# Sums on VectorE, products on GpSimd, and a shared ring of snapshots in a tuned RWKV-5 and SwiGLU kernel

## The chip, the cores and the metric

The kernel runs on one core of one Trainium2 chip. The metric is device time in microseconds (us) of one execution, lower is better. Each run below was judged against runs of the kernel before on the same chip, interleaved with it.

Engines are named as in the profile: PE is TensorE's matmul, PEld its weight load, DVE is VectorE, ACT is ScalarE, POOL is GpSimd, SP is SyncE.

## The reference

RWKV-5 attention over 4 batches, 8 heads, 768 tokens, head size 48, followed by a SwiGLU feed-forward block of width 384 to 1536 to 384 over the 3072 tokens:

```python
for t in range(S):                       # attention: one state per batch and head
    cur = u * k_t (outer) v_t
    y[t] = r_t @ (state + cur)
    state = w * state + k_t (outer) v_t
x = y.transpose(0, 2, 1, 3).reshape(B * S, H * D)
g = x @ w_gate
out = (g * sigmoid(g) * (x @ w_val)) @ w_out
```

(The einsums are written in words here.) The three weight matrices arrive as float64, which the kernel rounds to float32 itself.

## The kernel before

The tokens are cut into 24 units of 128. A unit `s` of the attention has `own_product` (r times k times u, on GpSimd) and `own_sum` (its sum over the head, on VectorE), which give the diagonal of a matrix `At`; `scale` makes the decayed k and r (`khat`, `rhat`), `turn` transposes them, `scores` fills `At`, `outputs` gives x, and `update` renews the state. While the first units run, 18 chunks of weights are rounded: ScalarE makes `w_mag` and `w_low`, VectorE joins sign and magnitude, GpSimd adds `w_low`.

```python
def round_pool():
    ...
    pool.tensor_tensor(dst, dst, low, ALU.add)

def own_product(i):
    kl, rl = k_ld[i % 2], r_ld[i % 2]
    rk = two.tile([P, H, D], FP32, name="rk", tag="rk")     # two buffers
    pool.tensor_mul(rk[:], rl[:], kl[:])
    pool.tensor_mul(rk[:], rk[:], ub[:])
    rks[i] = rk

def own_sum(i):
    dus[i] = three.tile([P, H], FP32, name="du", tag="du")
    dve.tensor_reduce(dus[i][:], rks.pop(i)[:], axis=AX.X, op=ALU.add)
```

The feed-forward block has two forms. The first four units go through plain matmuls into `gv` (gate and value). The rest goes, four units at a time, through a fast 2 by 2 matrix product that has seven block products instead of eight. It needs sums of its inputs (`s` of the weights, `hs` of the hidden activations `hT`), and copies of a PSUM accumulator taken between two products that are added up in it. Those copies are the **snapshots** `p1`, `u2` and `u3`; `c_a` and `c_b` are the accumulators of the first matmul of the block, `o_a` and `o_b` those of the second.

```python
def h_sums(g, n, by):                    # by: the engine
    h11, h12, h21, h22 = h_quarters(g)
    t = three.tile([P, 2, FH, P], FP32, name="hs", tag="w_bits")
    if n == 0:
        by.tensor_add(t[:, 0], h22, h21)
        by.tensor_sub(t[:, 1], t[:, 0], h11)
    else:
        by.tensor_sub(t[:, 0], h11, h21)
        by.tensor_sub(t[:, 1], h12, x["s"][1])
...
# four(g, f, what): one step of the first matmul, for one f of 128 hidden columns
if what in ("p1", "p6", "p7"):
    nm = {"p1": "p1", "p6": "u2", "p7": "u3"}[what]
    x[nm, f] = two.tile([P, 2 * P], FP32, name=nm, tag=nm)  # two buffers each
    act.copy(x[nm, f][:], ps)
...
if what == "h1":
    dve.tensor_mul(h[1], h[1], x.pop(("sg1", f))[:])
    dve.tensor_mul(h[1], h[1], x.pop(("u3", f))[:])         # last reader of u3
...
# two_projections: two of the four pairs of sums on GpSimd
if (j, p) in ((0, 1), (0, 2)):
    h_sums(g, p - 1, dve)
elif (j, p) in ((1, 1), (0, 3)):
    h_sums(g + 1, p // 3, pool)
```

The stage loop, with `gaps` filling in matmuls of the feed-forward block and the rounding of weights:

```python
for s in range(3, N + 2):
    if s + 1 < N:
        own_product(s + 1)
        scale(s + 1)
    if s < N:
        turn(s)
    gaps(s, 0)
    ...  # scores(s - 1), outputs(s - 2)
    if s < N:
        own_sum(s)
        diagonal(s)
    ...  # update(s - 2)
```

Of the kernel before, what the change touches and what calls it, by code (L numbers as in the profile page):

```python
# [15 lines left out]
P = 128  # L16
# [6 lines left out]
def fast(  # L23
# [33 lines left out]
    CC, FC = DM // P, DFF // P  # L57

    cst = ctx.enter_context(tc.tile_pool(name="cst", bufs=1))
    two = ctx.enter_context(tc.tile_pool(name="two", bufs=2))  # L60
    three = ctx.enter_context(tc.tile_pool(name="three", bufs=3))
    ps_a = ctx.enter_context(tc.tile_pool(name="ps_a", bufs=4, space=bass.MemoryType.PSUM))
    ps_w = ctx.enter_context(tc.tile_pool(name="ps_w", bufs=1, space=bass.MemoryType.PSUM))
    ps_f = ctx.enter_context(tc.tile_pool(name="ps_f", bufs=2, space=bass.MemoryType.PSUM))
# [135 lines left out]

    def own_product(i):
        kl, rl = k_ld[i % 2], r_ld[i % 2]
        rk = two.tile([P, H, D], FP32, name="rk", tag="rk")
        pool.tensor_mul(rk[:], rl[:], kl[:])
        pool.tensor_mul(rk[:], rk[:], ub[:])
        rks[i] = rk

    def own_sum(i):
        dus[i] = three.tile([P, H], FP32, name="du", tag="du")
        dve.tensor_reduce(dus[i][:], rks.pop(i)[:], axis=AX.X, op=ALU.add)  # L210


    sg0 = two.tile([P, 1], FP32, name="sg0", tag="sg0")
# [30 lines left out]
    for step, base in ((-64, 0), (64, D - 1)):  # L244
        pool.affine_select(
            out=own[:], in_=own[:], compare_op=ALU.is_ge, fill=0.0,
            base=base, pattern=[[step, 2]], channel_multiplier=1 if step < 0 else -1,
        )
    dve.tensor_scalar(held[:], wcol[:], W_LOW, W_HIGH, ALU.max, ALU.min)
    dve.tensor_copy(sq[:, 0, :], held[:])  # L250
    for l in range(1, 8):
# [4 lines left out]
    for l in range(7):  # L256
        n = 1 << l
        f = sq[:, l, :].unsqueeze(2).to_broadcast([P, HP, n])
        dve.tensor_mul(pw[:, :, P - 2 * n : P - n], pw[:, :, P - n : P], f)
    for n in (1, 0):  # L260
        t_ps = ps_a.tile([P, HP, P], FP32, name="t_ps", tag="a")
        for a in range(HP):
            pe.transpose(t_ps[:, a, :], pw[:, a, n : n + P], ident[:])
        x = t_ps[:].rearrange("p a (e x) -> p (a e) x", e=2)[:, :, 0:D]
        if n:
            act.copy(kscale[:], x)
        else:
            dve.reciprocal(rscale[:], x)
    own_product(0)
    own_product(1)  # L270
    own_sum(0)
    own_sum(1)

    pool.memset(mask[:], 1.0)
    pool.affine_select(
        out=mask[:], in_=mask[:], compare_op=ALU.is_gt, fill=0.0,
        base=0, pattern=[[1, P]], channel_multiplier=-1,
    )

    turned = {}  # L280
    small = deque()

    def scale(i):
        pool.tensor_mul(khat[i % 4][:, :, 0:D], k_ld[i % 2][:], kscale[:])
        pool.tensor_mul(rhat[i % 2][:, :, 0:D], r_ld[i % 2][:], rscale[:])
        if i >= 2:
            load_v(i)
        if i + 2 < N:
            load(i + 2)

    def diagonal(i):

        du = dus.pop(i)
        if i < 2:
            pool.tensor_mul(
                At[i][:], ident[:].unsqueeze(1).to_broadcast([P, H, P]),
                du[:].unsqueeze(2).to_broadcast([P, H, P]),
            )
        else:
            small.extend(  # L300
                lambda h=h: act.activation(  # L301
                    At[i % 2][:, h, :], ident[:], AF.Identity, scale=du[:, h : h + 1]
                )
                for h in range(H)
            )
# [84 lines left out]
    def gate_value(g, f):  # L390
        if f == 0:
            hT[g] = two.tile([P, FC, 2 * P], FP32, name="hT", tag="hT")
        gv = ps_f.tile([P, 2, 2 * P], FP32, name="gv", tag="gv")
        for o, wt in enumerate((wg, wv)):
            for c in range(CC):
                pe.matmul(  # L396
                    gv[:, o, :].rearrange("p (i t) -> p i t", i=2),
                    wt[:, c, P * f : P * (f + 1)], xT[:, 2 * g % NX : 2 * g % NX + 2, c, :],
                    start=(c == 0), stop=(c == CC - 1),
                )  # L400
        sg = two.tile([P, 2 * P], FP32, name="sg", tag="sg")
        act.activation(sg[:], gv[:, 0, :], AF.Sigmoid)
        dve.tensor_mul(sg[:], sg[:], gv[:, 0, :])
        dve.tensor_mul(hT[g][:, f, :], sg[:], gv[:, 1, :])  # L404
# [26 lines left out]
            hT[g][:, FH * k : FH * (k + 1), P * j : P * (j + 1)] for j in range(2) for k in range(2)  # L431
        ]

    def h_sums(g, n, by):
        h11, h12, h21, h22 = h_quarters(g)
        t = three.tile([P, 2, FH, P], FP32, name="hs", tag="w_bits")
        x = part_of.setdefault(g, {})
        x["s"] = x.get("s", ()) + (t[:, 0], t[:, 1])
        if n == 0:
            by.tensor_add(t[:, 0], h22, h21)  # L440
            by.tensor_sub(t[:, 1], t[:, 0], h11)  # L441
        else:
            by.tensor_sub(t[:, 0], h11, h21)
            by.tensor_sub(t[:, 1], h12, x["s"][1])

    def project(g, n):

        h11, h12, h21, h22 = h_quarters(g)
        x = part_of.setdefault(g, {})
        if n == 0:  # L450
            if g % 2 == 0:
                x["a"] = ps_o.tile([P, 2 * P], FP32, name="o_a", tag="o")[:, 0:NH]
                x["b"] = ps_w.tile([P, 2 * P], FP32, name="o_b", tag="w_mag")[:, 0:NH]
            else:
                x["a"], x["b"] = (
                    ps_f.tile([P, 2, 2 * P], FP32, name=n, tag="gv")[:, 0, 0:NH]
                    for n in ("o_a", "o_b")
                )
            x["out"] = [two.tile([P, DM], FP32, name=n, tag=n) for n in ("o_sb1", "o_sb2")]
        lhs, rhs, acc = (  # L460
            (h11, w11, "a"), (h12, w21, "b"), (1, wt[0], "a"), (2, wt[1], "a"),
            (0, w12, "b"), (h22, wt[2], "a"), (3, w22, "b"),
        )[n]
        if isinstance(lhs, int):
            lhs = x["s"][lhs]
        ps = x[acc]
        for f in range(FH):
            pe.matmul(  # L468
                ps, lhs[:, f, :], rhs[:, f, :],
                start=(f == 0 and n in (0, 1, 4)), stop=(f == FH - 1), skip_group_check=True,  # L470
            )
        o1, o2 = x["out"]
        if n in (0, 2, 3):
            nm = {0: "p1", 2: "u2", 3: "u3"}[n]
            x[nm] = two.tile([P, 2 * P], FP32, name=nm, tag=nm)[:, 0:NH]
            act.copy(x[nm], ps)  # L476
        elif n == 1:
            dve.tensor_add(o1[:, 0:NH], x["p1"], ps)
        elif n == 5:
            act.copy(o2[:, 0:NH], ps)  # L480
        elif n == 6:
            dve.tensor_add(o1[:, NH:DM], x["u2"], ps)  # L482
        if n in (3, 4):
            if "c22" in x:
                dve.tensor_add(o2[:, NH:DM], x["u3"], x["b"])
            x["c22"] = True
        if n >= 5:
            j = 6 - n
            c, b = divmod(2 * g + j, B)
            n0 = S * b + P * c  # L490
            act.dma_start(out=out[n0 : n0 + P, :], in_=x["out"][j][:])
# [47 lines left out]
    def four(g, f, what):  # L539
# [10 lines left out]
        h = [hT[g + j][:, f, :] for j in range(2)]  # L550
        if what in ("sg0", "sg1"):
            j = int(what[2])
            x[what, f] = two.tile([P, 2 * P], FP32, name="sg", tag="sg")
            act.activation(x[what, f][:], h[j], AF.Sigmoid)  # L554
            return
        if what == "h1":
            dve.tensor_mul(h[1], h[1], x.pop(("sg1", f))[:])  # L557
            dve.tensor_mul(h[1], h[1], x.pop(("u3", f))[:])  # L558
            return
        (w11, w12, w13), (s2, w22, w23) = (  # L560
            [w[:, c, P * f : P * (f + 1)] for c in range(CC)] for w in (wg, wv)
# [15 lines left out]
        )  # L577
        if what in ("p1", "p6", "p7"):
            nm = {"p1": "p1", "p6": "u2", "p7": "u3"}[what]
            x[nm, f] = two.tile([P, 2 * P], FP32, name=nm, tag=nm)  # L580
            act.copy(x[nm, f][:], ps)  # L581
        elif what == "c11":
            dve.tensor_add(h[0], x.pop(("p1", f))[:], ps)  # L583
# [21 lines left out]
    def two_projections(g):  # L605

        def item(j, p):
            if (j, p) in ((0, 1), (0, 2)):
                h_sums(g, p - 1, dve)
            elif (j, p) in ((1, 1), (0, 3)):  # L610
                h_sums(g + 1, p // 3, pool)
            elif (j, p) == (1, 3) and g + 2 < N // 2:
                w_sums(g + 2, 0)
            elif (j, p) == (1, 4) and g + 2 < N // 2:
# [51 lines left out]

    warm(14)

    round_act()
    scale(0)  # L670
    scale(1)
    turn(0)
    warm(3)
    turn(1)
    warm(3)
    diagonal(0)
    diagonal(1)
    scores(0)
    round_act()
# [3 lines left out]
    round_pool()  # L683
    own_product(2)
    scale(2)
    outputs(0)
    outputs(1)
    warm(4)
    queue(0)
    round_act()  # L690
    feed(1)
    round_act()
    round_pool()
    own_product(3)
    scale(3)
    feed(1)
    turn(2)
    dve.tensor_mul(
# [2 lines left out]
    )  # L701
    update(0)
    update(1)
    own_sum(2)
    round_weights()
    diagonal(2)
    for s in range(3, N + 2):
        if s + 1 < N:
            own_product(s + 1)
            scale(s + 1)  # L710
        if s < N:
            turn(s)
        gaps(s, 0)
# [8 lines left out]
            if s % 2:  # L722
                queue((s - 3) // 2)
        if s < N:
            own_sum(s)
            diagonal(s)
        if s >= 4:
            gaps(s, 3)
# [423 lines left out]
```

## Time and profile before

| kernel before | |
|---|---|
| median of 3 runs | 676.87 us (676.83 to 677.78) |
| span in the profile | 675.0 us |
| PE, DVE, POOL busy | 95%, 54%, 45% |
| early phase (up to the first `c_a` matmul) | 0 to 178.1 us |
| middle (first `c_a` to last `o_b` matmul) | 178.1 to 669.3 us: 491.2 us |
| four rounding stages between 51 and 104 us | 12.8, 12.4, 12.2, 11.8 us |

The last three rows are boundaries of my own, read from the tiles' start times, here rounded to 0.1 us: a stage lasts from one copy of `kT` on ScalarE to the next. The window of the middle (columns: start and end, length, then PE, PEld, DVE, ACT and POOL busy with instructions, granted clock, DMA share, GB/s):

```profile
178.10:669.30 491.20, 477.84 (x3154) 427.13 (x3153) 258.46 (x526) 164.87 (x460) 177.98 (x186) 1.00 0.07 18
```

PE is idle 491.20 - 477.84 = 13.4 us of it.

GpSimd's timeline around the same stage:

```profile
63.11 1.05 POOL L204 TENSOR_TENSOR rk<-r_ld,k_ld 128x384 f32<-128x384 f32 x1
...
67.18 1.95 POOL L192 TENSOR_TENSOR wg<-wg,w_low 128x768 int32<-128x768 int32 x1
...
73.75 1.84 POOL L192 TENSOR_TENSOR wo<-wo,w_low 128x768 int32<-128x768 int32 x1 [2.81 <-DMA w_bits<-in_moe_w_out_dram]
```

The product `rk` starts without a wait, and the weight addition, which frees one of the two buffers of `w_low` for ScalarE, starts 4.1 us after it. It ends at 69.13 us, 1.2 us before ScalarE writes `w_low` again. The 2.81 us of idle time stand further on, before the third addition.

### The profile page before, as it was taken

How to read it: one execution, taken by the hardware profiler on the slowest of the kernel's cores; microseconds unless marked ns; L12 is line 12 of the kernel's file. 1: busy time of each engine (PE TensorE's matmuls, PEld its weight loads, DVE VectorE, ACT ScalarE, POOL GpSimd, SP SyncE). 2: the span in 40 equal slices, each digit the busy share in tenths (PEclk: the TensorE clock that was granted, in tenths of full speed). 3: DMA queues.
4: the chain of work that ended last, by engine and by line, in shares of the span. 5: the costliest groups of instructions: out<-in, count | busy, mean ns of one | idle time of the engine just before them, and what ended most of it. 6: DMA issues, size and time to landing. Idle time of an engine off the chain costs nothing.

```text
span 675.0 us, 11983 instructions
## 1 busy us (share of the span) xinstructions
PE 644.1 (95%) x4702; PEld 573.8 (85%) x4702; DVE 365.8 (54%) x746; ACT 254.7 (38%) x678; POOL 306.2 (45%) x297
## 2 busy tenths in 40 slices
PE   8888999999999999989999999998999998999986
PEld 7777888899988899878899878888978888888886
DVE  6688774342366653386554365655256544465550
ACT  2568864343344432235340334442144320234300
POOL 5888779458554308266034724404412004531040
PEclk9998999999999999999999999999999999999999
DMA  8898931323110102011010200000100000000001
GB/s 208 216 254 227 249 79 36 61 48 68 51 25 13 24 1 48 36 36 36 1 35 14 70 1 13 14 2 1 48 1 0 2 1 13 36 0 1 1 2 51
DMA packets 85779, 34.11 MB, mean 51 GB/s; under 512 B 76368, under 2 KB 79568, under 8 KB 85712
## 3 DMA queue, kind: packets, MB, share of 16 engines
q1 hardware_dynamic: 82256, 28.52, 18.1%
q10 hardware_dynamic: 3456, 4.72, 1.9%
q8 instruction: 39, 0.64, 0.4%
q14 instruction: 28, 0.23, 0.1%
HBM read 28.51 MB, written 4.72 MB: 49 GB/s over the span
## 4 chain that ended last, share of the span: by engine, by line
PE 77%; DVE 12%; ACT 4%; POOL 3%; issue 2%; DMA 1%; SPq 0%; ACTq 0%; DVEq 0%; POOLq 0%
PE c_b L574 21%; PE c_a L574 18%; PE o_a L468 13%; PE o_b L468 9%; PE gv L396 4%; PE y_ps L358 4%; PE s_ps L327 3%; PE tp L314 2%; PE u_ps L371 2%; DVE hs L441 1%; DVE hT L557 1%; DVE hT L558 1%; ACT At L301 1%; DVE hT L585 1%; ACT w_mag L164 1%
## 5 line engine op out<-in xcount | busy, mean ns | idle before, releaser
L385 POOL TENSOR_TENSOR Z<-Z,wL 112x384 f32<-112x384 f32 x16 | 19.1, 1191 | 132.2 <-DVE Z L384 132.2
L581 ACT COPY u<-c_a 128x256 f32<-128x256 f32 x120 | 44.6, 372 | 90.8 <-PE c_a L574 82.2
L574 PE MATMUL c_a<-t,wv 128*128 128x256 f32 x240 | 73.5, 388 | 5.3 <-ACT u L581 3.6
L574 PE MATMUL c_b<-xT,wg 128*128 128x256 f32 x240 | 71.5, 379 | 0.0
L554 ACT ACTIVATE sg<-hT 128x256 f32<-128x256 f32 x120 | 50.2, 418 | 52.3 <-DVE hT L583 36.6
L301 ACT ACTIVATE At<-ident,du 128x128 f32<-128x128 f32 x176 | 61.9, 399 | 11.9 <-DVE o_sb L482 8.0
L588 DVE TENSOR_TENSOR u<-u,c_b 128x256 f32<-128x256 f32 x60 | 25.2, 420 | 70.9 <-PE c_b L574 55.4
L574 PE MATMUL c_b<-xT,s 128*128 128x256 f32 x240 | 62.4, 379 | 0.0
L534 POOL TENSOR_TENSOR s<-wv,wg 128x256 f32<-128x256 f32 x24 | 17.6, 735 | 87.4 <-PE c_b L574 64.6
L574 PEld LDWEIGHTS c_a<-t,wv 128*128 128x128 f32 x240 | 43.6, 190 | 15.8 <-ACT u L581 5.6
L468 PE MATMUL o_a<-wt,hs 128*128 128x192 f32 x288 | 50.6, 328 | 6.1 <-DVE hs L441 6.1
L468 PEld LDWEIGHTS o_a<-wt,hs 128*128 128x128 f32 x288 | 46.8, 190 | 7.2 <-issue 7.1
L332 DVE COPY_PREDICATED At<-mask,s_ps 128x512 f32<-128x512 int32 x48 | 32.5, 731 | 35.0 <-ACT At L301 25.9
L468 PE MATMUL o_b<-wo,hs 128*128 128x192 f32 x288 | 51.1, 327 | 0.0
L574 PEld LDWEIGHTS c_b<-xT,wg 128*128 128x128 f32 x240 | 45.5, 190 | 6.4 <-DVE hT L590 0.2
L574 PEld LDWEIGHTS c_b<-xT,s 128*128 128x128 f32 x240 | 45.3, 190 | 6.5
L440 POOL TENSOR_TENSOR hs<-hT 128x768 f32<-128x768 f32 x6 | 12.6, 2093 | 81.5 <-DVE hT L558 81.5
L468 PEld LDWEIGHTS o_b<-wo,hs 128*128 128x128 f32 x288 | 47.2, 190 | 0.7 <-issue 0.6
L358 PE MATMUL y_ps<-At,v_ld 128*32 128x128 f32 x768 | 35.3, 273 | 6.1 <-ACT kT L316 3.4
L583 DVE TENSOR_TENSOR hT<-p,c_b 128x256 f32<-128x256 f32 x60 | 25.1, 419 | 28.7 <-PE c_b L574 25.4
L476 ACT COPY u<-o_a 128x192 f32<-128x192 f32 x24 | 7.7, 319 | 82.9 <-PE o_a L468 72.9
L396 PE MATMUL gv<-xT,wg 128*128 128x256 f32 x144 | 37.8, 400 | 1.0 <-DVE hT L404 1.0
(120 smaller groups left out, 1466.0 us busy)
## 6 DMA issues: line engine op xcount, KB each, us to landing
k_ld<-in_k_dram SPq DMA_DIRECT2D x24, 192.0 KB, 2.9
r_ld<-in_r_dram SPq DMA_DIRECT2D x24, 192.0 KB, 3.6
w_bits<-in_moe_w_gate_dram SPq DMA_DIRECT2D x6, 768.0 KB, 5.5
v_ld<-in_v_dram SPq DMA_DIRECT2D x48, 96.0 KB, 2.6
w_bits<-in_moe_w_val_dram SPq DMA_DIRECT2D x6, 768.0 KB, 5.6
w_bits<-in_moe_w_out_dram SPq DMA_DIRECT2D x6, 768.0 KB, 5.3
out_dram<-o_sb ACTq DMA_DIRECT2D x24, 192.0 KB, 1.9
ub<-in_u_dram SPq DMA_DIRECT2D x1, 192.0 KB, 4.0
```

The source lines that it names most:

```text
L301: lambda h=h: act.activation(At[i % 2][:, h, :], ident[:], AF.Identity, scale=du[:, h : h + 1])
L327: pe.matmul(ps[e][:, a, :], kT[i % 2][rows, a, :], turned[i][rows, a, :], start=True, stop=True, skip_group_check=True,)
L332: dve.copy_predicated(At[i % 2][:].rearrange("p (a e) t -> p a e t", e=2)[:, :, e], mask[:].bitcast(INT32).unsqueeze(1).to_broadcast([P, H ...
L358: pe.matmul(ps[32 * q : 32 * q + 32, cc, :], *rows[q][n], start=(n == 0), stop=(n == len(rows[q]) - 1), skip_group_check=True,)
L385: pool.tensor_mul(z[0:R2], z[0:R2], w)
L396: pe.matmul(gv[:, o, :].rearrange("p (i t) -> p i t", i=2), wt[:, c, P * f : P * (f + 1)], xT[:, 2 * g % NX : 2 * g % NX + 2, c, :], start ...
L468: pe.matmul(ps, lhs[:, f, :], rhs[:, f, :], start=(f == 0 and n in (0, 1, 4)), stop=(f == FH - 1), skip_group_check=True,)
L554: act.activation(x[what, f][:], h[j], AF.Sigmoid)
L574: pe.matmul(ps.rearrange("p (i t) -> p i t", i=2), lhs, rhs, start=first, stop=what not in ("p2", "p5", "p4", "p3"), skip_group_check=True,)
L581: act.copy(x[nm, f][:], ps)
L583: dve.tensor_add(h[0], x.pop(("p1", f))[:], ps)
L588: dve.tensor_add(x["u3", f][:], x["u3", f][:], ps)
```

## The change

The intent: (1) all sums `hs` go to VectorE, so that VectorE and GpSimd no longer hold each other up; (2) the product with `u3` goes to GpSimd in exchange; (3) the three pairs of snapshot buffers become one ring of seven, and `sg` gets a third buffer; (4) to make room, `rk` has one buffer instead of two (unit 1 borrows `At[1]`), and `own_sum` moves from the end of a stage to its beginning; (5) the first unit's work is reordered: the mask early, its own product first, k scaled as soon as its scale is there, the reciprocal in halves, its diagonal on ScalarE.

```diff
+    one = ctx.enter_context(tc.tile_pool(name="one", bufs=1))
+    seven = ctx.enter_context(tc.tile_pool(name="seven", bufs=7))
...
     def own_product(i):
-        rk = two.tile([P, H, D], FP32, name="rk", tag="rk")
+        if i == 1:
+            rk = At[1][:, 0:3, :]...            # (rearranged)
+        else:
+            rk = one.tile([P, H, D], FP32, name="rk", tag="rk")[:]
...
+    own_product(0)
     for n in (1, 0):
...
         if n:
             act.copy(kscale[:], x)
+            own_sum(0)
         else:
-            dve.reciprocal(rscale[:], x)
-    own_product(0)
-    own_product(1)
-    own_sum(0)
-    own_sum(1)
+            for h in (slice(0, HP), slice(HP, H)):
+                dve.reciprocal(rscale[:, h], x[:, h])
...
-        sg = two.tile([P, 2 * P], FP32, name="sg", tag="sg")
+        sg = three.tile([P, 2 * P], FP32, name="sg", tag="sg")
...
-    def h_sums(g, n, by):
+    def h_sums(g, n):                           # by.* became dve.*
...
-            x[nm] = two.tile([P, 2 * P], FP32, name=nm, tag=nm)[:, 0:NH]
+            x[nm] = seven.tile([P, 2 * P], FP32, name=nm, tag="part")[:, 0:NH]
...
-            dve.tensor_mul(h[1], h[1], x.pop(("u3", f))[:])
+            pool.tensor_mul(h[1], h[1], x.pop(("u3", f))[:])
...
-            x[nm, f] = two.tile([P, 2 * P], FP32, name=nm, tag=nm)
+            x[nm, f] = seven.tile([P, 2 * P], FP32, name=nm, tag="part")
...
+    scale_k(0)
+    diagonal(0)
+    for _ in range(H):
+        small.popleft()()
     round_act()
-    scale(0)
-    scale(1)
+    scale_k(1)
+    scale_r(0)
+    load_next(0)
     turn(0)
+    scale_r(1)
+    own_product(1)
+    own_sum(1)
+    load_next(1)
...
     queue(0)
+    own_sum(2)
...
     update(1)
-    own_sum(2)
     round_weights()
     diagonal(2)
     for s in range(3, N + 2):
+        if s < N:
+            own_sum(s)
         if s + 1 < N:
             own_product(s + 1)
...
         if s < N:
-            own_sum(s)
             diagonal(s)
```

## The prediction

> **What bounds the kernel now.** I read the page's busy table first, then the chain that ended last:
>
> ```profile
> PE 644.1 (95%) x4702; PEld 573.8 (85%) x4702; DVE 365.8 (54%) x746; ACT 254.7 (38%) x678; POOL 306.2 (45%) x297
> ...
> PE 77%; DVE 12%; ACT 4%; POOL 3%; issue 2%; DMA 1%; SPq 0%; ACTq 0%; DVEq 0%; POOLq 0%
> ```
>
> The first line is busy time by engine, the second the shares of the chain. TensorE is busy 95% of the span and carries 77% of the chain; the other engines are half empty. The change removes no matmul, so all it can win is TensorE idle time: 675.0 - 644.1 = 30.9 us. Next I cut the span into windows (columns: PE, PEld, DVE, ACT, POOL busy) to see where that idle time lies:
>
> ```profile
> 0.00:10.00 10.00, 7.13 (x39) 6.94 (x40) 5.76 (x29) 1.49 (x2) 3.30 (x12) 1.00 0.61 122
> ...
> 50.00:75.00 25.00, 21.77 (x170) 18.48 (x171) 19.98 (x44) 19.38 (x47) 18.91 (x15) 0.93 0.90 237
> ...
> 100.00:125.00 25.00, 25.00 (x249) 21.51 (x248) 9.62 (x20) 9.84 (x28) 20.20 (x15) 1.00 0.22 43
> ...
> 450.00:500.00 50.00, 47.83 (x371) 44.12 (x370) 20.10 (x37) 12.95 (x37) 16.15 (x16) 1.00 0.04 16
> ...
> 650.00:675.00 25.00, 19.59 (x121) 19.30 (x119) 2.88 (x7) 1.91 (x6) 3.58 (x2) 0.95 0.10 36
> ```
>
> Summing all the windows: 12.1 us idle before 100 us, 5.4 us after 650 us (the last stores, not touched), the rest, 13.4 us, between 100 and 650. The view of TensorE's waits names them:
>
> ```profile
> PE o_a L468 <- DVE hs L441: 6.1, 4, 1.8
> PE c_a L574 <- ACT u L581: 3.6, 5, 0.8
> ...
> PE c_b L574 <- DVE hT L583: 2.0, 3, 1.3
> PE c_a L574 <- ACT p L581: 1.5, 3, 0.8
> ```
>
> These four (total us, times, longest) sum to 13.2 of the 13.4 us. So the middle of the run is explained by four kinds of wait, and the change aims at the first two. Why does "hs" come late? The timeline near the end shows it:
>
> ```profile
> 644.33 0.95 DVE L440 TENSOR_TENSOR hs<-hT 128x768 f32<-128x768 f32 x1
> 644.58 2.37 POOL L440 TENSOR_TENSOR hs<-hT 128x768 f32<-128x768 f32 x1 [27.97 <-DVE hT L558]
> 645.31 2.44 DVE L441 TENSOR_TENSOR hs<-hs,hT 128x768 f32<-128x768 f32 x1
> 647.02 2.41 POOL L441 TENSOR_TENSOR hs<-hs,hT 128x768 f32<-128x768 f32 x1
> ...
> 647.90 2.19 PE L468 MATMUL o_a<-wt,hs 128*128 128x192 f32 x12 [1.80 <-DVE hs L441]
> ```
>
> The first sum on VectorE takes 0.95 us, the second, of the same size, 2.44 us: it stands still until GpSimd's sum is through. TensorE pays 1.80 us. And why does the copy "u" come late? ScalarE's timeline:
>
> ```profile
> 398.12 0.37 ACT L581 COPY u<-c_a 128x256 f32<-128x256 f32 x1 [1.93 <-DVE hT L558]
> ```
>
> The copy waits for L558, the last product that reads the old snapshot u3: its buffer is not free. The waits in short windows show this wait of TensorE exactly once in each of the five blocks of products (0.7, 0.5, 0.7, 0.8, 0.8 us). It comes where the second and third f of a block start: by the kernel's table, u3 of f=2 is written at step 25 and u3 of f=0 released at step 24.5.
>
> **What the Trainium skill says.** "SBUF — State Buffer", section "Who interferes with whom": a VectorE instruction with two SBUF inputs and a GpSimd instruction that reads SBUF exclude each other, and the second to issue waits for the whole of the first. This trace agrees: the 128x768 sum is 946 ns where it has the port alone, 2443 ns at the median of L441. "GPSIMD Engine Reference", section 3.1: elementwise work costs about 1.96 times VectorE's. Here 1807 against 946 ns for 768 elements, 0.73 against 0.42 us for 256. "Perfetto Trace Analysis", section "Optimization Strategy": a repeating gap can mean too few buffers; the gap once per block is one.
>
> **The change part by part.**
>
> 1. *Sums of hT all on VectorE.* Removed from GpSimd: 6 x (2.09 + 2.21 + 1.81 + 1.82) = 47.6 us. Added to VectorE: 24 x 0.95 = 22.8 us, not on the path: the third needed sum has four groups of 12 matmuls (about 1.95 us each) ahead of it. What counts is the first pair. At 644 us: L557 ends at 643.95; then L440 0.95, one product on GpSimd holding the port for about 0.55, L441 0.85, so hs is ready near 646.3 instead of 647.75. TensorE was ready at 647.90 - 1.80 = 646.1. So 1.8 us of wait becomes about 0.2. The pair near 460 us gains more still (VectorE's own_sum no longer stands in front of it) and the 0.7 us wait at 357 us goes. Of 6.1 us I take 5.2 away.
>
> 2. *Product with u3 (L558) on GpSimd.* VectorE loses 60 x 0.536 = 32.2 us, GpSimd gains 60 x 0.73 = 44 us: GpSimd's load ends nearly where it was (306 - 48 + 44 - 2 = 300 us), VectorE's at about 356. No matmul reads the result soon, but it now releases the snapshot from behind GpSimd's queue, where a unit's four products (about 4 us), a state product (1) and four weight sums (2.9) can run in a row.
>
> 3. *Ring of seven snapshots, three sg.* By the step table, with seven in rotation u3 of f=2 takes the slot of u2 of f=0, released at step 18, 7 steps before 25. A step is 0.43 us (six instructions in 1.29 us, two to a step), so 3 us of slack instead of 0.2. The 3.6 us wait should nearly go: 3.3. In the steady part p1 takes u3's slot of three f earlier, 8.5 steps or 3.7 us after its release, plus 4 steps before TensorE needs the copy. This absorbs most of a GpSimd queue, not all: I charge 1.0 us for the first block, where weight sums have six operations, and 0.5 for the others.
>
> 4. *Waits on L583 and p.* A VectorE with 9 us less to do and its own_sum moved ahead wins a little of the 3.5 us; the 1.3 us one comes from a VectorE product that a GpSimd train held for 3.45 us, and that train stays. I take 0.8.
>
> 5. *First unit.* VectorE: own_sum about 9.7, halves of the reciprocal 10.8 to 13.4. GpSimd scales k at 10.9 instead of 12.5 and r is done near 14.0 instead of 14.5; the diagonal goes to ScalarE, eight at 0.30 us, 10.9 to 13.3, pushing its first w_mag from 12.2 to 13.2. The copies kT, rT wait for w_mag's second half, behind L182: 16.2 instead of 16.9. So scores start some 0.7 us earlier. But rk now has one buffer, and own_sum(2) stands on VectorE before the rounding of the third chunk: VectorE must wait for GpSimd's product near 27.5, and L182, at 27.4 before, comes near 28.9. That takes the 0.7 us back.
>
> 6. *own_sum at a stage's beginning.* In the rounding stages (40 to 98 us) the chain runs through VectorE, ScalarE and GpSimd, 12.45 us a stage, with 0.46 us of own_sum in it. Moving it into VectorE's slack (1.2 us before L332) can save this per stage, while GpSimd's next own_product, which must wait for it, starts about 3 us later (50.4 to 53.4) and its weight additions with it; those had 2.8 to 3.1 us idle before them. I take parts 5 and 6 together as -0.3 us.
>
> Sum: -5.2 - 3.3 + 1.5 - 0.8 - 0.3 = -8.1 us: 676.9 - 8.1 = 668.8 us, 1.2% less.
>
> **The rivals.** *GpSimd's queue becomes a wait:* snapshots come free late, ScalarE stands still on a copy, and TensorE with it. For it: VectorE instructions held 1.1 and 3.4 us by trains of GpSimd work at 288 to 296 us, and a first block where GpSimd is busy 16.1 of 25 us. Against it: GpSimd has 45% load and slack of 3.7 us plus four steps. If each block lost 1.5 us beyond my charge, 7.5 us, all would be lost: about 676. *The early stages decide:* TensorE idles 6 us between 30 and 98 us and runs warm-up matmuls before; if the earlier first unit and own_sum shorten the chain by 0.5 us a stage, 664 to 666; if GpSimd waiting for own_sum delays the weights, 2 to 3 us worse, 671 to 672. *The gain is only moved:* hs ready in time, but VectorE now blocks at the fourth pair of sums, whose buffer comes free only after a later group of matmuls, delaying outputs; against it, no TensorE work waits for these soon.
>
> **Range and chances.** The two sure waits give -8.5; the doubtful terms are about +-2.5 each way in the early stages and up to +4 from GpSimd's queue. The range is 664.8 to 673.2. Faster by over 2% needs under 663.3, that is 13.5 us, more than all idle time in the middle: 5%. Slower by over 2% needs a new bottleneck: 1%.
>
> **What would show it.** TensorE's waits: hs from 6.1 to under 1.5 us, ACT u from 3.6 to under 0.8; GpSimd about 300 us busy; L441 on VectorE near 1 to 1.5 us. First gv matmul still near 27 us (27.37 before), and TensorE saturated from about 98 us as before. Wrong would be: waits of TensorE on snapshot copies with GpSimd's product as releaser, or a first saturated window displaced by over 2 us.

## More of the kernel before

To a hundredth the middle goes from 178.13 to 669.27 us, 491.14 us.

The copies that bound one rounding stage, in ScalarE's timeline (start, duration, engine, line, operation, tile):

```profile
65.16 0.57 ACT L316 COPY kT<-tp 128x512 f32<-128x512 f32 x1
...
70.31 0.93 ACT L168 ACTIVATE w_low<-w_bits 128x768 int32<-128x768 uint32 x1
...
77.52 0.58 ACT L316 COPY kT<-tp 128x512 f32<-128x512 f32 x1
```

That stage takes 77.52 - 65.16 = 12.36 us.

## The result and the profile after

| | before | after |
|---|---|---|
| median, same chip | 677.19 us (676.83 to 680.14, 5 runs) | 666.27 us (665.80 to 667.09, 5 runs) |
| span in the profile | 675.0 us | 665.3 us |
| first `gv` matmul | 27.4 us | 27.4 us |
| early phase | 178.1 us | 181.1 us |
| middle | 491.1 us | 478.5 us |
| rest | 5.7 us | 5.7 us |

The ratio is 0.9832, with a 95% interval of 0.9810 to 0.9854: 1.7% faster. A ratio here is the mean time of one kernel's runs over that of the other's of the same rounds, so it is not quite the ratio of the medians in the table.

After the change the middle goes from 181.06 to 659.54 us. The three phases add up to the difference of the spans: +2.93 - 12.65 + 0.00 = -9.72 us. So the middle won more than the whole profiled run did. The early phase lost something, but a part of its 2.93 us is chance (see the clock, below). The page of the changed kernel, busy time and chain:

```profile
PE 643.7 (97%) x4702; PEld 575.7 (87%) x4702; DVE 352.6 (53%) x711; ACT 257.9 (39%) x686; POOL 303.2 (46%) x333
...
PE 85%; DVE 8%; ACT 3%; issue 2%; DMA 0%; DVEq 0%; SPq 0%; ACTq 0%
```

PE has the same 4702 matmuls and its share of the chain rose from 77% to 85%: other engines hold it up less. TensorE's waits (total us, times, longest):

```profile
PE gv L410 <- DVE hT L418: 4.0, 3, 2.2
...
PE c_a L588 <- ACT p L595: 1.6, 3, 0.8
...
PE c_b L588 <- DVE hT L597: 0.9, 1, 0.9
```

Of the four waits of the middle that the prediction counted, "hs" (6.1) and "ACT u" (3.6) are gone from the list. What stands first now is a wait of the early phase, `gv`, which was 1.0 us before. The windows of a stage that rounds weights, of the steady part and of the whole middle:

```profile
50.00:75.00 25.00, 20.10 (x166) 17.00 (x167) 21.13 (x40) 19.16 (x46) 17.76 (x14) 1.00 0.78 223
...
450.00:500.00 50.00, 49.58 (x378) 45.71 (x377) 21.96 (x44) 14.42 (x41) 11.74 (x16) 1.00 0.05 17
...
181.10:659.50 478.40, 475.56 (x3153) 427.56 (x3152) 237.76 (x486) 165.58 (x460) 183.12 (x226) 1.00 0.08 19
```

In the steady window PE's busy time rose from 47.83 to 49.58 of 50 us. In the early one it fell from 21.77 to 20.10 of 25 us, which shows little by itself: the kernel before had a stretch of half clock in that window (0.93 against 1.00), where each matmul is busy for longer, and the matmuls are nearly as many (170 and 166). In the whole middle PE's idle time fell from 13.4 to 2.8 us, by 10.5, and the busy time of the same matmuls (3154 and 3153 records) fell by 2.1, taken between the boundaries to a hundredth (2.3 in the rounded windows shown). Together these are the 12.7 us. The timeline near the end, where the first pair of `hs` had stood still:

```profile
635.68 0.95 DVE L454 TENSOR_TENSOR hs<-hT 128x768 f32<-128x768 f32 x1
635.84 1.38 POOL L572 TENSOR_TENSOR hT<-hT,u 128x256 f32<-128x256 f32 x1 [0.70 <-DVE hT L571]
636.66 1.37 DVE L455 TENSOR_TENSOR hs<-hs,hT 128x768 f32<-128x768 f32 x1
...
638.18 2.19 PE L482 MATMUL o_a<-wt,hs 128*128 128x192 f32 x12
```

The second sum takes 1.37 us where it took 2.44; it stands still a little, 0.42 us, beside GpSimd's product, the one that the change put there, which runs until 637.22. TensorE's matmul carries no wait any more.

Where the early phase lost: all engines' waits between 40 and 102 us.

```profile
POOL rk L210 <- DVE du L216: 13.9, 5, 3.4
...
ACT w_low L170 <- POOL wg L194: 3.1, 2, 1.9
```

Neither line exists before. ScalarE's timeline in the stage that took 12.36 us:

```profile
65.50 0.58 ACT L330 COPY kT<-tp 128x512 f32<-128x512 f32 x1
...
72.76 0.93 ACT L170 ACTIVATE w_low<-w_bits 128x768 int32<-128x768 uint32 x1 [1.88 <-POOL wg L194]
...
79.33 0.58 ACT L330 COPY kT<-tp 128x512 f32<-128x512 f32 x1
```

And GpSimd's:

```profile
66.93 1.02 POOL L210 TENSOR_TENSOR rk<-r_ld,k_ld 128x384 f32<-128x384 f32 x1 [3.41 <-DVE du L216]
...
70.91 1.81 POOL L194 TENSOR_TENSOR wg<-wg,w_low 128x768 int32<-128x768 int32 x1
```

The stage lasts 13.83 us. The product waits 3.41 us for VectorE's `own_sum`, because that sum reads the one buffer of `rk`; the weight addition stands behind it in GpSimd's order, 5.4 us after the start of the stage (70.91 - 65.50) where it was 2.0 us before (67.18 - 65.16); and ScalarE waits 1.88 us for the `w_low` that the addition frees. The four stages are 14.3, 13.8, 13.3 and 11.8 us.

**The clock.** Each profile has one to three stretches of TensorE at half speed in the first 75 us, at varying places: before at 50 to 60 us, after at 20 to 30 us, each with a mean granted clock of 0.83 over 10 us, which is what 3.4 us at half speed makes. The Trainium skill, "TensorE: Matmul & The Clock Gate", Part 1, says that the clock has only the two states, half and full, and that the activity window of some 3.4 us is free-running, so the place differs from run to run. The traces agree: the stretches at half speed last 3.4 us (24.17 to 27.58 in the changed kernel) or 6.8 us (24.41 to 31.23 in e3). I therefore do not explain a difference of under 2 us in the early phase from one profile alone.

How much the place of a stretch can do is seen in e2 below. It comes to the first `c_a` with the rounding stages of the kernel before, but has a stretch at 25.8 to 29.2 us, where the kernel before has none until 54.6. Its copy of `kT` near 34 us comes 2.0 us later than before, and so does its first `c_a` matmul (180.12 against 178.13 us). Against e2 the changed kernel, with its stretch at 24.2 to 27.6 us, reaches `c_a` 0.9 us later (181.06). So some 2 of the 2.93 us are probably the clock of that one run. A stretch in the rounding stages costs nothing that shows: e5 has one at 51.6 to 55.0 us and reaches `c_a` at 181.03 us.

### The profile page after: what moved, and what is told of

Same layout as the page of the kernel before. It is cut to its first block, busy times and chain, and to the rows that moved or that the text cites. A ratio compares the mean times of both kernels' runs of the same rounds, so it can differ in the third digit from the quotient of the medians.

```text
span 665.3 us, 12005 instructions
## 1 busy us (share of the span) xinstructions
PE 643.7 (97%) x4702; PEld 575.7 (87%) x4702; DVE 352.6 (53%) x711; ACT 257.9 (39%) x686; POOL 303.2 (46%) x333
## 4 chain that ended last, share of the span: by engine, by line
PE 85%; DVE 8%; ACT 3%; issue 2%; DMA 0%; DVEq 0%; SPq 0%; ACTq 0%
PE c_b L588 23%; PE c_a L588 20%; PE o_a L482 14%; PE o_b L482 11%; PE y_ps L372 5%; PE gv L410 4%; PE s_ps L341 3%; PE tp L328 2%; PE u_ps L385 2%; ACT At L315 1%; DVE wo L183 1%; DVE At L346 1%; PE warm L245 1%; DVE hT L418 1%; DVE wv L183 1%
## 5 line engine op out<-in xcount | busy, mean ns | idle before, releaser
L572 POOL TENSOR_TENSOR hT<-hT,u 128x256 f32<-128x256 f32 x60 | 47.0, 784 | 174.0 <-DVE hT L571 152.5
L315 ACT ACTIVATE At<-ident,du 128x128 f32<-128x128 f32 x184 | 64.3, 396 | 9.3 <-DVE o_sb L496 8.0
L399 POOL TENSOR_TENSOR Z<-Z,wL 112x384 f32<-112x384 f32 x16 | 21.4, 1339 | 56.3 <-DVE Z L398 56.3
L595 ACT COPY p<-c_a 128x256 f32<-128x256 f32 x60 | 22.3, 372 | 40.3 <-PE c_a L588 35.3
```

The lines of the kernel that those rows point to most:

```text
L315: lambda h=h: act.activation(At[i % 2][:, h, :], ident[:], AF.Identity, scale=du[:, h : h + 1])
L399: pool.tensor_mul(z[0:R2], z[0:R2], w)
L572: pool.tensor_mul(h[1], h[1], x.pop(("u3", f))[:])
```

## The experiments

Theory A, formed after the result: the middle's gain is the sum of several removed waits, and the early loss comes from `own_sum` moved ahead together with the single `rk` buffer. Rival B: the early loss comes from the first unit's new order or from chance of the clock. Rival C: the product on GpSimd brings nothing or costs something, as the prediction charged. Eleven runs were made (e5 is the changed kernel once more), on three chips (e1 to e4, e5 to e8, e9 to e11), all correct against the reference. The medians and ratios are against the kernel before on the same chip (679.33, 677.57 and 678.04 us).

| run | four stages, us | last `gv` starts | middle, us | median, us | ratio, 95% |
|---|---|---|---|---|---|
| before | 12.8 12.4 12.2 11.8 | 135.0 | 491.1 | 677.19 | 1 |
| after | 14.3 13.8 13.3 11.8 | 137.9 | 478.5 | 666.27 | 0.9832 (0.9810 to 0.9854) |
| e1 before, own_sum early, one rk | 14.3 13.8 13.3 11.8 | 141.1 | 487.9 | 678.16 | 0.9991 (0.9971 to 1.0010) |
| e2 before, all sums on VectorE | 12.7 12.4 12.2 11.8 | 137.0 | 485.4 | 672.25 | 0.9902 (0.9879 to 0.9925) |
| e3 before, ring of six | 12.8 12.4 12.2 11.8 | 137.6 | 486.3 | 672.21 | 0.9902 (0.9882 to 0.9923) |
| e4 after, second rk | 14.2 13.1 12.8 11.8 | 135.7 | 478.5 | 664.79 | 0.9798 (0.9777 to 0.9820) |
| e5 after, again | 14.4 13.8 13.3 11.8 | 137.9 | 478.5 | 666.37 | 0.9820 (0.9802 to 0.9839) |
| e6 after, second rk, own_sum late | 12.7 12.4 12.2 11.8 | 133.4 | 478.5 | 663.84 | 0.9785 (0.9765 to 0.9805) |
| e7 after, first unit as before | 14.4 13.9 13.3 11.8 | 139.7 | 478.5 | 668.57 | 0.9852 (0.9832 to 0.9873) |
| e8 after, u3 product on VectorE | 14.3 13.8 13.3 11.8 | 137.2 | 479.6 | 667.42 | 0.9841 (0.9823 to 0.9859) |
| e9 after, three pairs | 14.4 13.8 13.3 11.8 | 137.6 | 488.1 | 674.74 | 0.9943 (0.9922 to 0.9964) |
| e10 after, ring of six, two sg | 14.4 13.9 13.3 11.8 | 137.5 | 479.2 | 666.92 | 0.9833 (0.9816 to 0.9851) |
| e11 e10, two rk, own_sum late | 12.8 12.4 12.2 11.8 | 133.7 | 478.3 | 663.61 | 0.9787 (0.9766 to 0.9808) |

The stages repeat to within 0.2 us between kernels that share an order of `own_sum` and a number of `rk` buffers, and the middle of the changed kernel repeats to 0.1 us (478.5 both times). The start of the last `gv` does not: it carries the clock's stretches.

The four stages leave something out. Where `own_sum` is early, the two stages just before them are shorter. From the third copy of `kT` (near 34 us) to the ninth (near 102 us), over six stages, it is 67.9 us in the kernel before, e2, e3, e6 and e11; 70.2 to 70.5 in the changed kernel, e5 and e7 to e10; 70.7 in e1; and 68.5 in e4.

### e1: only the part that makes room, on the kernel before

```diff
-        rk = two.tile([P, H, D], FP32, name="rk", tag="rk")
+        rk = At[1]... if i == 1 else one.tile([P, H, D], FP32, name="rk", tag="rk")[:]
...
     for s in range(3, N + 2):
+        if s < N:
+            own_sum(s)
...
-            own_sum(s)
             diagonal(s)
```

(and `own_sum(2)` before the rounding, as in the change)

> The kernel before with one thing taken from the change: one rk buffer, so own_sum moves to a stage's start and GpSimd's next own_product waits for it. Theory A (the single rk buffer costs the early stages about 3 us in the changed kernel): GpSimd waits about 14 us for du between 40 and 102 us, ScalarE's w_low waits for GpSimd, the rounding stages grow from 12.45 to about 13.8 us, the last gv matmul starts near 138 us instead of 135.0, and the time is 679 to 681 us, 0.3 to 0.6% above the kernel before. Theory B (the loss comes from the reordered first unit and the place of the half-speed stretch of the clock): the stages stay at 12.4 us and the time is 676 to 678 us.

Measured: ratio 0.9991, no change in all, but its two halves moved apart. The stages became 14.3, 13.8, 13.3 us, as long as in the changed kernel, although none of its other parts is there. GpSimd's timeline in one of them:

```profile
70.12 1.01 POOL L208 TENSOR_TENSOR rk<-r_ld,k_ld 128x384 f32<-128x384 f32 x1 [3.41 <-DVE du L214]
```

This is the wait of the changed kernel, 3.41 us and all. So the loss in the stages is this part's, and rival B falls for them. Over six stages the loss is 2.7 us. Against e3, whose clock has the same stretch at 24.4 to 31.2 us, the first `c_a` comes 3.5 us later (184.26 and 180.75 us). The middle became 3.2 us shorter, which theory A had not expected, and that is why its expected time was missed. TensorE's waits show where:

```profile
PE o_a L472 <- DVE hs L445: 4.6, 3, 1.8
...
PE c_a L578 <- ACT u L585: 3.1, 4, 0.8
...
PE c_b L578 <- DVE hT L587: 1.0, 2, 0.6
```

Against before, `hs` has 1.5 us less, "ACT u" 0.5 and "DVE hT" 1.0: with `own_sum` out of VectorE's way there, VectorE is ready earlier where TensorE needs it.

### e2: only the sums on VectorE, on the kernel before

```diff
-                h_sums(g + 1, p // 3, pool)
+                h_sums(g + 1, p // 3, dve)
```

> The kernel before with one thing taken from the change: all sums of hT on VectorE. Theory A: TensorE's wait for hs (6.1 us in four) falls under 1 us, and [...]the gain is 5.5 to 7.5 us: 669.5 to 671.5 us. Rival (the wait moves to what VectorE does next, as it blocks on the fourth pair): under 3 us gained, 674 to 677 us, with new waits of TensorE on VectorE.

Measured: ratio 0.9902, the middle 485.4 us, 5.8 less. TensorE's waits:

```profile
PE c_a L574 <- ACT u L581: 3.6, 5, 0.8
...
PE o_a L468 <- DVE hs L441: 0.6, 2, 0.3
```

The wait on `hs` fell from 6.1 to 0.6 us, that on `u` stayed at 3.6. The two waits are independent, and the 5.5 us of one became 5.8 us of time. The median lies above the 669.5 to 671.5 us expected, on a chip where the kernel before is slower too; the gain lies inside the 5.5 to 7.5 us of theory A.

### e3: only a shared ring, on the kernel before

```diff
+    six = ctx.enter_context(tc.tile_pool(name="six", bufs=6))
...
-            x[nm, f] = two.tile([P, 2 * P], FP32, name=nm, tag=nm)
+            x[nm, f] = six.tile([P, 2 * P], FP32, name=nm, tag="part")
```

(and the same in the second matmul)

> The kernel before with one thing: the snapshots p1, u2, u3 share one ring of six buffers (the same memory as three pairs), the product with u3 stays on VectorE. Theory A (the wait is u3 of the third f of a block falling on the slot of u3 of the first f): TensorE's wait on ScalarE's copy u goes from 3.6 us in five to under 0.8 us, gain 3 to 5 us: 672 to 674 us. Rival (it is the late product itself, whatever the slot; or seven are needed): wait stays over 2 us, 675 to 677.5 us.

The ring here has six buffers, exactly as much memory as the three pairs, so this measures the sharing and not the seventh buffer. Measured: ratio 0.9902, the middle 486.3 us, 4.8 less. TensorE's waits:

```profile
PE o_a L469 <- DVE hs L442: 6.2, 4, 1.8
...
PE c_b L575 <- DVE hT L584: 2.0, 3, 1.3
PE c_a L575 <- ACT p L582: 1.5, 3, 0.8
```

There is no line for "ACT u" any more, and the other three are as before. The removed 3.6 us in five waits brought 4.8 us. The view of waits by weight loads had put the same five at 5.6 us in the kernel before: the loads run ahead of the matmuls and so stood still longer. The measured gain lies between the two figures.

### e4: the changed kernel with a second rk for the early stages

```diff
         if i == 1:
             rk = At[1]...
+        elif i in (3, 5, 7):
+            rk = wt[2][:, 0:2, :]...            # not yet in use at this time
         else:
             rk = one.tile(...)
```

> The changed kernel with a second rk buffer in the early stages (units 3, 5, 7 use a weight-sum tile that is not yet in use), own_sum at the start of a stage as in the change. Theory A (single rk): GpSimd's waits for du between 40 and 102 us vanish, w_low no longer waits, stages of 12.0 to 12.5 us, the last gv near 134 us instead of 137.9; time 662 to 663.5 us. Theory B (first unit or clock): no gain, 665.5 to 667 us.

A plain second buffer does not fit beside a ring of seven and three `sg` (5.84 KB a partition are left where the ring needs 7), so odd units borrow a tile for weight sums that is empty until later. Measured: 664.79 us, ratio 0.9798. The waits of GpSimd's product on `own_sum` and of `w_low` on GpSimd's additions are gone between 40 and 102 us. But the second and third stages are 13.1 and 12.8 us: shorter than the 13.8 and 13.3 of the changed kernel, longer than the 12.4 and 12.2 of before, and the first one did not move (14.2). The four sum to 51.9 us, against 53.3 in the changed kernel and 49.1 before: counted so, the second buffer took back a third of the loss. Over all six stages it took back 1.7 of 2.3 us (68.5, 70.2 and 67.9), which is nearer to what the ratios say (0.9798 against 0.9832 and 0.9820). The time missed the 662 to 663.5 us of theory A, and the stages its 12.0 to 12.5: theory A, which put all of the loss on the wait for `rk`, was incomplete.

### e5: the changed kernel again

> The changed kernel again, for a comparison on the same chip as the next three. Both theories: 0.983 of the kernel before, within 0.003; first c_a to last o_b 478.4 us within 0.3; stages of 13.8 and 13.3 us in the rounding part.

Measured: 666.37 us, ratio 0.9820, a middle of 478.5 and stages of 14.4, 13.8, 13.3 us. This profile had two stretches at half clock in the early phase where the first had one, and the same span of 665.3 us. It is the yardstick for e6 to e8, which ran on its chip.

### e6: e4, with own_sum back at the end of the early stages

```diff
     for s in range(3, N + 2):
-        if s < N:
+        if 8 <= s < N:
             own_sum(s)
...
         if s < N:
+            if s < 8:
+                own_sum(s)
             diagonal(s)
```

(and `own_sum(2)` back to its old place, after `update(1)`)

> The changed kernel with a second rk buffer for units 3, 5, 7 and own_sum back at the end of a stage up to stage 7 (early only after that). Theory A (the early stages lose 4.2 us because GpSimd's work starts late behind own_sum, and VectorE's order with it): the stages return to 12.4 and 12.2 us, no wait of GpSimd for du, time 3 to 4.5 us under the changed kernel on the same chip, so 0.977 to 0.9785 of the kernel before, and under the variant with the early own_sum (0.9798). Theory B (the loss that was left in that variant, 13.1 and 12.8 us a stage, comes from something else in the change, such as the ring): no better than 0.9798.

Measured: 663.84 us, ratio 0.9785, 2.5 us less than the changed kernel on the same chip, where theory A had 3 to 4.5. ScalarE's timeline, one stage:

```profile
63.61 0.57 ACT L333 COPY kT<-tp 128x512 f32<-128x512 f32 x1
...
75.98 0.58 ACT L333 COPY kT<-tp 128x512 f32<-128x512 f32 x1
```

75.98 - 63.61 = 12.37 us: the stage of the kernel before to a hundredth, and the middle keeps its 478.5. Since e4 and e6 differ only in the place of `own_sum`, the early place by itself lengthens the first three stages by 1.4, 0.7 and 0.6 us. It also shortens the two stages before them, by 0.9 and 1.2 us, so that over the six stages it costs only 0.7 us (68.54 against 67.88). By what path it does so stays open. In e4's trace the VectorE instruction right after `own_sum`, the first step of rounding a half chunk, takes 1.23, 1.02 and 1.11 us where the same one often takes 0.42, beside GpSimd's scaling of k and r. The 26 such steps from the copy of `kT` near 39 us to the one near 101 us take 15.6 us in e6 and 15.7 before, but 18.2 in e4 and 19.6 in the changed kernel. That this is the cause was not tested. In total time e4 and e6 are not told apart: their intervals overlap, and they ran on different chips. Only the stages tell them apart.

### e7: the changed kernel without the first unit's new order

```diff
-    own_product(0)
     for n in (1, 0):
...
-            for h in (slice(0, HP), slice(HP, H)):
-                dve.reciprocal(rscale[:, h], x[:, h])
+            dve.reciprocal(rscale[:], x)
+    own_product(0)
+    own_product(1)
+    own_sum(0)
+    own_sum(1)                                   # mask after these, too
...
-        if i == 1:
+        if i < 2:                                # diagonal(0) on GpSimd
```

> The changed kernel with the whole first-unit part undone (order of the first unit as before), everything else kept. My prediction's step 5: the first unit's 0.7 us are given back, so the time is within 0.7 us of the changed kernel. Rival (the first unit is worth what the copy kT near 51 us shows, 1.25 us earlier than before, or more): 1 to 2.5 us slower than the changed kernel, 0.985 to 0.987 of before.

Measured: 668.57 us against 666.37 on the same chip, ratio 0.9852 against 0.9820: without it the kernel is 2.2 us slower. The middle is the same (478.5). So the first unit's order is worth about 2 us, and the prediction's reason for "given back" does not hold. The two ratios' intervals overlap a little (0.9832 to 0.9873 and 0.9802 to 0.9839), the times themselves do not (667.92 and more, 667.06 and less), so the size is less sure than the sign. In the profiles, which have two half-speed stretches each before 60 us, the first `c_a` comes at 182.85 us against 181.03. The start of the first `gv` is 28.8 us here against 27.3 in e5. In the first profile of the changed kernel it lies at 27.4, as before, although its first `y_ps` starts at 20.09 us against 21.14: there the half clock fell into the window from 20 to 30 us.

### e8: the changed kernel with the product by u3 back on VectorE

```diff
-            pool.tensor_mul(h[1], h[1], x.pop(("u3", f))[:])
+            dve.tensor_mul(h[1], h[1], x.pop(("u3", f))[:])
```

> The changed kernel with the product with u3 back on VectorE, ring of seven and all sums on VectorE kept. Theory A (the product's place is worth little: in the run with only the sums moved, the wait for hs was already down to 0.6 us): first c_a to last o_b 478 to 479.5 us, time within 1 us of the changed kernel. Rival (VectorE needs the relief of 32 us of work): TensorE waits for VectorE's hs or hT over 2 us more, 2 to 4 us slower.

Measured: 667.42 us against 666.37, ratio 0.9841 against 0.9820; the middle 479.6 against 478.5. TensorE waits 0.6 us for `hs` again. So the product on GpSimd saves some 1.1 us. Rival C falls: I had charged +1.5 for it. The middle is 0.1 us over what theory A allowed. The two ratios' intervals overlap; it is the middle, which repeats to 0.1 us, that carries the reading.

### e9: the changed kernel with three pairs instead of the ring

```diff
-            x[nm, f] = seven.tile([P, 2 * P], FP32, name=nm, tag="part")
+            x[nm, f] = two.tile([P, 2 * P], FP32, name=nm, tag=nm)
```

> The changed kernel with the ring undone: p1, u2 and u3 have two buffers each again, while the product with u3 stays on GpSimd. Theory A (u3's slot of two f earlier is released half a step before it is wanted, and on GpSimd the release comes later still): TensorE's wait on ScalarE's copy u is back at 3.5 us or more, first c_a to last o_b 483 to 487 us instead of 478.4, time 5 to 8 us above the changed kernel, 0.990 to 0.994 of the kernel before. Rival (the sums and own_sum had taken the wait away already): middle under 480 us, 0.983 to 0.985.

Measured: 674.74 us, ratio 0.9943, the middle 488.1 us. The wait which the prediction feared from GpSimd's queue is here. ScalarE's timeline:

```profile
231.40 0.37 ACT L594 COPY u<-c_a 128x256 f32<-128x256 f32 x1 [4.00 <-POOL hT L571]
```

The copy of a snapshot waits 4.00 us for GpSimd's product, because with a pair of buffers that product has to release one. In all ScalarE waits 12.7 us in seven copies, and TensorE 4.8 us in six, up to 2.8 us at once. Around this longest one, from 220 to 240 us, the mean granted clock is 0.83 (6.8 us at half speed, so some 3.4 us of time), the only such stretch between 180 and 650 us in any trace here; it is part of the 488.1, and whether the stall caused it was not tested. The ring, worth 4.8 us in the kernel before (there with six buffers), is worth 9.6 us of the profile's middle (488.1 - 478.5), or some 6 without the slow clock, once the product is on GpSimd. The middle is longer than the 483 to 487 us of theory A by less than that slow stretch. The two parts belong together.

### e10: the changed kernel with a ring of six and two sg

```diff
-    seven = ctx.enter_context(tc.tile_pool(name="seven", bufs=7))
+    seven = ctx.enter_context(tc.tile_pool(name="seven", bufs=6))
...
-        sg = three.tile([P, 2 * P], FP32, name="sg", tag="sg")
+        sg = two.tile([P, 2 * P], FP32, name="sg", tag="sg")
```

> The changed kernel with a ring of six snapshots instead of seven and two sg buffers instead of three: 2 KB per partition less. Theory A (sharing one ring is what removes the wait; the seventh buffer and the third sg are only slack): first c_a to last o_b 478 to 479.5 us, time within 1 us of the changed kernel, 0.982 to 0.984 of the kernel before. Rival (with the product on GpSimd the slack is needed): waits of TensorE on copies u or p over 3 us, 2 to 5 us slower.

Measured: 666.92 us, ratio 0.9833, the middle 479.2 us. The seventh buffer and the third `sg` together are worth 0.7 us in the middle, at 2 KB a partition, which the second buffer of `rk` could have had.

### e11: e10 with two rk, and own_sum late in the early stages

```diff
-            rk = one.tile([P, H, D], FP32, name="rk", tag="rk")[:]
+            rk = two.tile([P, H, D], FP32, name="rk", tag="rk")[:]
```

(and `own_sum` placed as in e6)

> The memory freed by a ring of six and two sg buffers is spent on a plain second rk buffer for all units, and own_sum stands at a stage's end up to stage 7 and at its start after that. Theory A: rounding stages of 12.4 and 12.2 us as before, middle 478.4 to 479.5 us, 662.5 to 664.5 us, 0.977 to 0.9795 of the kernel before, the same as the variant with the borrowed tile. Rival (one of the two buffers given up is needed): middle over 481 us, no better than the changed kernel, 0.982 or more.

Measured: 663.61 us, ratio 0.9787, stages of 12.8, 12.4, 12.2 and 11.8 us, a middle of 478.3. It is 14.4 us under the kernel before and 3.3 us under e10, both on the same chip; its interval does not overlap with e10's (0.9766 to 0.9808, 0.9816 to 0.9851). The changed kernel did not run on this chip; by the ratios e11 is faster than it too (0.9787 against 0.9832 and 0.9820), though the interval of e5 overlaps. It is level with e6 and needs no borrowed tile.

## Why the prediction was right or wrong

The time was right: 666.3 us lies in the range from 664.8 to 673.2 and 2.5 us from the middle value, and "within 2%" was the likely class. But the total came out of errors in both directions, so that it came so near is in part luck. The sum, term by term; "measured" is the single experiment that isolates the part, in the middle of the profile unless said otherwise:

| step of the prediction | predicted, us | measured, us | from |
|---|---|---|---|
| 1 sums on VectorE | -5.2 | -5.8 | e2 |
| 3 ring | -3.3 | -4.8 | e3 |
| 2, 3 product on GpSimd, its queue | +1.5 | -1.1 | e8 against after |
| 4 waits on L583 and p | -0.8 | -1.0 | 3.5 to 2.5 in TensorE's waits |
| 5 first unit | with 6: -0.3 | -2.2, in time | e7 against e5 |
| 6 own_sum early, one rk: six stages | with 5: -0.3 | +2.7 (+4.2 in the last four) | e1 |
| 6 own_sum early: middle | in part 1 and 4 | -3.2 | e1 |

1. **Sums on VectorE: right.** The wait, the path and nearly the size. The second sum fell from 2.44 to a median of 1.16 us, inside the 1 to 1.5 foretold.
2. **The product with u3: the busy times were right, the effect was not.** GpSimd was foretold at 300 us and has 303.2, VectorE at 356 and has 352.6. The charge of 1.0 us for the first block and 0.5 for the others is the step that failed: no wait of TensorE on a snapshot behind GpSimd is left in the changed kernel. The slack of 3.7 us and four steps, which the prediction had worked out for the ring, was enough; e9 shows that the mechanism is real where the slack is missing. The last line of the prediction's "wrong would be" did not come about on this point.
3. **The ring: mechanism right, size too small.** The term was TensorE's wait of 3.6 us, taken at 3.3. It measured 4.8: removing the wait won more than the gap that the matmul's line shows. Why was not tested.
4. **The small waits: right in size.** But e1 shows that `own_sum` out of the way does this, together with 1.5 us of `hs`; so it overlaps with step 1. The single effects -5.8, -4.8, -3.2 and -1.1 sum to -14.9, and together the parts brought -12.7.
5. **The first unit: wrong.** "That takes the 0.7 us back" was argued from one collision on VectorE near 27.5 us. That step failed in both its terms. The gain is larger: the first copy of `kT` comes at 15.60 us instead of 16.87, 1.3 us earlier and not 0.7. And the collision is smaller: VectorE does wait for GpSimd's product, 2.72 us, but the product had come earlier too, and the rounding step behind it (27.43 us before) starts at 27.90 us and not near 28.9. e7 measured a gain of about 2 us that is kept.
6. **own_sum and rk: the mechanism was seen, the size was wrong.** The prediction had GpSimd's product start about 3 us later; it waits 3.4 us. The failing step is the next clause, that the weight additions "had 2.8 to 3.1 us idle before them". In the kernel before that idle time stands before the third addition of a stage (2.81 us at 73.75); the first, at 67.18 us, follows GpSimd's scaling without a wait. ScalarE's `w_low` stands behind that first addition, with 1.2 us to spare (69.13 to 70.31). A delay of 3.4 us is more than that, so ScalarE waited (1.88 us in the stage shown), and three stages grew by 1.6, 1.5 and 1.1 us. In e1 the early phase lost about 3 us by it (2.7 over six stages, 3.5 against e3). The changed kernel's early phase ended 2.9 us later in the profile, beyond the 2 us that the prediction itself named as a sign of being wrong, though some 2 of them are probably the clock's. e4 and e6 show that the buffer and the place of the sum each have a share in it: 1.7 and 0.7 us over the six stages.

Of the rivals, "the gain is only moved" did not happen, and "the early stages decide" was half right: GpSimd waiting for `own_sum` did delay the weights, by about 3 us as it said (e1), but the middle gave 12.7 us where the prediction's terms for it (steps 1 to 4) gave 7.8. The two errors of the profiled pair, +3.2 early and -4.9 in the middle, left 1.7 us of the span's difference. Without the clock's 2 us the early error would be near +1.2: the loss of about 3 us in step 6 and the gain of about 2 in step 5, both missed, nearly cancel.

## What to carry to other kernels

When a change moves work between two engines that hold each other up, cut the run into phases by tile start times and judge each part in the phase where it acts; an unchanged total (e1) can hide a gain and a loss of the same size. Before you take a buffer away to pay for another, check which engine's order stands behind the one that will wait for it: here a second `rk`, with `own_sum` left at the end of the early stages, was worth more than the seventh snapshot and the third `sg` together (e11, e10). Moving the last reader of a buffer to a slower engine is safe only with enough buffers in rotation, so test those two parts together.

## What the Trainium skill lacked or had wrong

- "SBUF — State Buffer", section "Who interferes with whom", says that the second to issue is blocked for the whole of the first instruction. In the kernel before a VectorE product was held for a whole train of GpSimd instructions, one after the other. The timeline of VectorE and GpSimd:

```profile
287.44 1.00 POOL L385 TENSOR_TENSOR Z<-Z,wL 112x384 f32<-112x384 f32 x1 [11.95 <-DVE Z L384]
288.04 3.45 DVE L585 TENSOR_TENSOR hT<-hT,sg 128x256 f32<-128x256 f32 x1
288.40 0.73 POOL L534 TENSOR_TENSOR s<-wv,wg 128x256 f32<-128x256 f32 x1
...
290.45 0.73 POOL L537 TENSOR_TENSOR s<-wg,wv 128x256 f32<-128x256 f32 x1
```

  The product, 0.42 us by itself, was issued at 288.04 and ended at 291.49, and four weight sums of about 0.73 us went ahead of it. Near 645 us, on the other hand, the two engines' sums alternated. When a waiting VectorE instruction gets its turn, the page does not say.
- "GPSIMD Engine Reference", section 3.1, gives a ratio of 1.96 to VectorE for 2048 elements. Here it is 1.91 for 768 (1807 against 946 ns) and about 1.74 for 256 (0.73 against 0.42 us), so the ratio is not the same for short rows.
- I found no page that says how much time is won when a wait of TensorE that this profile shows is removed. Here five waits that the matmuls show as 3.6 us and the weight loads as 5.6 us were worth 4.8 us (e3), and in the whole middle 10.5 us less idle time made 12.7 us, the rest being 2.1 us less busy time of the same matmuls.
